# A gated recurrence feeding a balanced mixture of experts: the first expert's list apart, weights behind its rows, transposes ahead, matmuls dealt anew

## The chip, the cores and the metric

One core of a Trainium2 chip runs the whole kernel in one launch. The metric is the device time of an execution in microseconds (us); lower is better. The engines are named as in the profile: PE is TensorE's matmul (PEld its weight load), DVE is VectorE, ACT is ScalarE, POOL is GpSimd, and SP is the sync engine, which here issues loads from HBM.

## The reference

A gated linear recurrence over 4 batches, 8 heads, 768 tokens and head size 48 gives 3072 tokens of width 384. A layer of 8 experts follows, in which each token goes to exactly one expert and each expert takes exactly 384 tokens. All values are float32.

```python
f = 1.0 / (1.0 + np.exp(-f_logit))
for t in range(S):
    state = f[:, :, t, :, None] * state + np.einsum('bhd,bhe->bhde', k[:, :, t], v[:, :, t])
    y[:, :, t] = np.einsum('bhd,bhde->bhe', q[:, :, t], state)
x = y.transpose(0, 2, 1, 3).reshape(B * S, H * D)

logits = x @ w_gate                       # 3072 x 8
order = np.argsort(-logits.flatten())
for idx in order:                         # greedy: highest logit first
    tok, e = (int(idx) // E, int(idx) % E)
    if assigned[tok] >= 0 or counts[e] >= cap:     # cap = 3072 // 8 = 384
        continue
    assigned[tok] = e
    counts[e] += 1
for e in range(E):
    mask = assigned == e
    h = np.maximum(x[mask] @ w1[e], 0.0)  # 384 x 1024
    out[mask] = h @ w2[e]                 # 1024 x 384
```

## The kernel before

**Attention.** The recurrence is worked in 24 chunks of 128 tokens, as a software pipeline of seven stages (`attention`). The last stage, `gate`, computes a chunk's 8 logits and writes the row (384 outputs and 8 logits) to the DRAM tensor `xd`. SP loads the inputs of the chunks. SP's order is not written by hand; a scheduler places its instructions, while the orders of PE, DVE, ACT and POOL are written by hand in the expert phase (`tc.manual_schedule`).

**First list.** `search` finds, by 4 digits of 31 thresholds each, which tokens are above an expert's capacity bound for their first choice: DVE compares (`above`), PE counts (`cnt`), DVE takes the fullest expert (`most`, `filled`), and PE turns that into the next `base`. `positions` numbers the tokens within each expert, and `sort` produces the lists: DVE builds `numb` (which list column a token belongs to, times its number; 30 columns of 24) and `in_line` (which line of the list, in three parts), and 24 matmuls multiply them into `tokens`. The column order is 6 columns of left-over tokens (NL) and 3 per expert (TE). The result is rounded to integers in `tok`. `idle_turns(n)` puts n matmuls on a tile of ones into the PE queue whose result nobody reads.

**Gathers.** `fetch(e, i)` gathers the 128 rows of list column i of expert e from `xd` by an indirect DMA of POOL (196 KB, L534). POOL issues the two of expert 0, then six small gathers of the left-over tokens' logits (`lg`, L653), then two for each of experts 1 to 4.

**Weights.** `load_weights(e, ...)` issues w1 and w2 of an expert on SP (1536 KB each; L422 and L424). Experts 0 and 1 have space of their own (`early`) and are called for near the end of attention. Experts 2 to 4 use space that attention gives back. Experts 5 to 7 take over the tiles of experts 0 to 2 and are called for from the piece queue.

**Experts and routing side by side.** The left-over tokens are assigned in seven further rounds of `search`, whose chain runs back and forth between DVE and PE. Expert matmuls fill PE in between. An expert part (`ffn(e, first_block, n)`) is a list of pieces: n `turn`s (three transposes of gathered rows into a PSUM bank `Xe`, then an ACT copy to `xeT`, L486), 24 `up`s (three accumulate into a bank `H`, then an ACT Relu to `hT`, L498) and 8n `down`s (eight accumulate into `O`, then an ACT copy to `o`, L510, and POOL's scatter to the output, L511). `Xe` and `H` share three PSUM banks. Pieces wait in the deque `pe_work`, in the order of the parts: two blocks of each of experts 0 to 4, later the third blocks of these, then experts 5 to 7 whole.

The dealing is done when the program is built. A pair of clocks stands for PE and DVE. `V` adds an estimated DVE cost; `PE` is called ahead of each routing matmul, and first takes pieces as long as PE's clock stands behind DVE's:

```python
        def PE(cost):
            while pe_work and clock["pe"] + 0.2 < clock["dve"]:
                piece()
            clock["pe"] = max(clock["pe"], clock["dve"] + 0.05) + cost
            clock["dve"] = max(clock["dve"], clock["pe"] + 0.1)
```

When the lists are complete, a flag `beyond` is read by the engines (L762); it tells whether a general path must redo the work, which these inputs don't need. The remaining pieces then follow without routing between them.

Of the kernel before, what the change touches and what calls it, by code (L numbers as in the profile page):

```python
# [24 lines left out]
def kernel(  # L25
# [272 lines left out]
    def tt(out_, a, b, op):  # L298
        nc.vector.tensor_tensor(out=out_, in0=a, in1=b, op=op)
# [119 lines left out]

    def load_weights(e, pool, slot):  # L420
        w1 = pool.tile([128, DC, F], FP32, name="w1", tag=f"w1_{slot}", bufs=1)
        nc.sync.dma_start(out=w1[:], in_=moe_w1[e].rearrange("(c p) f -> p c f", p=128))  # L422
        w2 = pool.tile([128, FC, D], FP32, name="w2", tag=f"w2_{slot}", bufs=1)
        nc.sync.dma_start(out=w2[:], in_=moe_w2[e].rearrange("(c p) d -> p c d", p=128))  # L424
        slots[e] = (w1, w2)
# [3 lines left out]
    bounds(NCH - 1)  # L429
    overs(0, B, 0, NCH - 1)  # L430
    attention(ALL - 4, ALL - 1)
    load_weights(0, early, 0)
    first_choices(0, B - 1, NCH - 1, NCH)
    overs(0, B - 1, NCH - 1, NCH)
    attention(ALL - 1, ALL)
    load_weights(1, early, 1)
    first_choices(B - 1, B, NCH - 1, NCH)
# [5 lines left out]
    def fast():  # L443
# [12 lines left out]

        def V(cost=0.17):
            clock["dve"] += cost

        def PE(cost):  # L460
            while pe_work and clock["pe"] + 0.2 < clock["dve"]:
                piece()
            clock["pe"] = max(clock["pe"], clock["dve"] + 0.05) + cost
            clock["dve"] = max(clock["dve"], clock["pe"] + 0.1)

# [7 lines left out]
        def ffn(e, first_block, n):  # L473
# [27 lines left out]
            def down(i, ft):  # L501
                def go():
# [14 lines left out]

            return ([turn(i) for i in range(n)]
                    + [up(ft, d) for ft in range(FC) for d in range(DC)]
                    + [down(i, ft) for i in range(n) for ft in range(FC)])  # L520

        rows, lists = {}, {}

        def place_of(e, i):
            return NL + TE * (E - 1 - e) + i
# [13 lines left out]
        def search(over, choice, n, held):  # L539

            base = bank("base", "b")
            for d in range(DIGITS):
                above = rt([n, TH], f"above{n}", FP16)
                a, s = last_of(over, TH), mid_of(steps[d][:], n)
                if d == 0:
                    tt(above[:], a, s, ALU.is_ge)
                else:
                    stt(above[:], a, base[:, 0:1], s, ALU.subtract, ALU.is_ge)
                V(0.12 + n * TH / 960)
                r = bank("cnt", "r")  # L550
                PE(0.03 * n + 0.1)
                for c in range(n):
                    nc.tensor.matmul(out=r[0:TH, 0:E], lhsT=above[:, c, :], rhs=choice[:, c, :],  # L553
                                     start=(c == 0), stop=(c == n - 1 and held is None))
                if held is not None:
                    nc.tensor.matmul(out=r[0:TH, 0:E], lhsT=ones16[:, 0:TH], rhs=held[:],
                                     start=False, stop=True)
                most, filled = rt([1], "most"), rt([1], "filled", FP16)
                reduce(most[0:TH], r[0:TH, 0:E], ALU.max)
                ts(filled[0:TH], most[0:TH], CAP - 0.5, ALU.is_ge)  # L560
                V(0.35)
                PE(0.06)
                nc.tensor.matmul(out=base[:, 0:1], lhsT=units[d][0:TH, :], rhs=filled[0:TH],
                                 start=(d == 0), stop=(d == DIGITS - 1), skip_group_check=True)
            return base

        def positions(kind, nk, n, code, notfirst_, held):
# [9 lines left out]
                                         op0=ALU.mult, op1=ALU.add)  # L577
            V(0.1 + w / 400)
            PE(0.2)
# [13 lines left out]
            stt(line[:], q[:], -128.0, pos[:], ALU.mult, ALU.add)  # L593
            tt(blk[:], q[:], code, ALU.add)
            return total, line, blk

        def sort(line, blk, val, blocks_, n, nq, part):

            numb = rt([nq, n], f"numb{n}", FP16)
            tt(numb[:], mid_of(blk[:], nq), blocks_, ALU.is_equal)  # L600
            tt(numb[:], numb[:], mid_of(val, nq), ALU.mult)
            V(0.2 + nq * n / 960)
            r = bank("tokens", "r")
            in_line = rt([n // 2, 128, 2], f"in_line{n}", FP16, 1)
            lp = line[:].rearrange("p (c j) -> p c j", j=2)
            for c0 in range(0, n // 2, part):
                tt(in_line[:, c0:c0 + part], lp[:, c0:c0 + part].unsqueeze(2).to_broadcast(
                    (128, part, 128, 2)), mid_of(pairs[:], part), ALU.is_equal)
                V(0.12 + part * 256 / 1900)
                PE(0.03 * 2 * part)  # L610
                for c in range(2 * c0, 2 * (c0 + part)):
                    nc.tensor.matmul(out=r[:, 0:nq], lhsT=in_line[:, c // 2, :, c % 2],
                                     rhs=numb[:, :, c], start=(c == 0), stop=(c == n - 1))
            return r

# [9 lines left out]
        with tc.manual_schedule(engines=engines):  # L625
# [10 lines left out]
            idle_turns(12)  # L636
            r = sort(line, blk, value[:], blocks[:], NT, NQ, 4)
            idle_turns(6)
            found, tok = rt([NQ], "found", FP32, 1), rt([NQ], "tok", I32, 1)
            ts(found[:], r[:, 0:NQ], -1024.0, ALU.max, 2047.0, ALU.min)  # L640
# [3 lines left out]
               float(1024 * (DX // E) + D // E), ALU.add)  # L644
            for e in range(NA):
                for i in range(2):
                    p = place_of(e, i)
                    lists[e, i] = tok[:, p:p + 1]
            fetch(0, 0)
            fetch(0, 1)  # L650
            lg = rt([NL, E], "lg", FP32, 1)
# [9 lines left out]

            clock.update(pe=6.0, dve=0.0)
            for e in range(NA):
                if e >= 2:
                    load_weights(e, pools[e], e)
                pe_work.extend(ffn(e, 0, 2))

# [14 lines left out]
            nc.vector.memset(got[:], 0.0)  # L682
            clock["dve"] = 14.0
            ts(lg[:], lg[:], low_scale[:, 0:1], ALU.add, low_scale[:, 1:2], ALU.mult)
            tt(lg[:], lg[:], last_of(gone[:], E), ALU.add)
            for rnd in range(1, E):
# [3 lines left out]
                tt(ch[:], lg[:], last_of(ov[:], E), ALU.is_equal)  # L690
                V(0.55)
# [4 lines left out]
                V(0.4)  # L696
                if rnd == E - 1:
# [3 lines left out]
                tt(now[:], held[:], more[:], ALU.add)  # L701
                V(0.35)
                PE(0.1)
                m2 = bank("m2", "r")
# [5 lines left out]
                tt(lg[:], lg[:], last_of(gone[:], E), ALU.add)  # L710
                V(0.7)

# [4 lines left out]
            tt(kind2[:], mid_of(code2[:], E), kinds[:, 1:KC, 0:NL], ALU.is_equal)  # L717
            V(0.6)
# [4 lines left out]
            r = sort(line2, blk2, val_l[:], blocks[:, NL:NQ, 0:NL], NL, NQ - NL, 3)  # L723
            tok2 = rt([NQ - NL], "tok2", I32, 1)
# [4 lines left out]
            for e in range(E):  # L729
                for i in range(2 if e < NA else 0, TE):  # L730
                    p = place_of(e, i) - NL
                    lists[e, i] = tok2[:, p:p + 1]
            ends = bank("ends", "r")
            nc.tensor.matmul(out=ends[:, 0:E], lhsT=ones16[:], rhs=total[:, 1:KC], start=True,
# [8 lines left out]
            reduce(twice[:], times[:], ALU.max)  # L743
            stt(span[:], twice[:], 1.5, span[:], ALU.is_ge, ALU.add)
            nc.tensor.matmul(out=ends[:, E:E + 1], lhsT=onesf[:], rhs=span[:], start=True,
                             stop=True)
# [599 lines left out]
```

## Time and profile before

| | |
|---|---|
| median of 3 runs | 510.9 us (507.04 to 511.99) |
| the profiled execution | 509.44 us, span from first to last instruction 507.5 us |
| PE busy | 460.7 us, 91% of the span |
| DVE, ACT, POOL busy | 156.4, 135.8, 106.3 us |
| mean granted TensorE clock | 0.965 |
| weight loads | 16 of 1536 KB on SP |

Times in the views count from the span's first instruction. "Busy" of PE is the time in which at least one matmul is under way. In the profile's slices each digit is a share in tenths of one fortieth of the span (12.7 us); "PEclk" is the clock granted to TensorE. A view of the timeline gives start, duration, engine, line, operation and the tiles written and read, and in brackets how long the engine was idle before and what ended that. A view of waits gives the waiting engine and line, then what it waited for, with total time, number of times and the longest.

### The profile page before, as it was taken

To read this page: it belongs to the slowest core of one execution; us is meant where nothing else is said; L and a number is where in the kernel's file an instruction comes from. 1 tells how busy PE (TensorE), PEld (TensorE's weight loads), DVE (VectorE), ACT (ScalarE), POOL (GpSimd) and SP (SyncE) were. 2 spreads that over 40 slices of the span, in tenths; PEclk is the share of its full clock that TensorE was granted. 3 is DMA by queue.
4 is the path that set the end of the run, shared out by engine and by line. 5 is a ranking of instruction groups with operands and counts; after the bars stand their busy time and mean duration, and the time that the engine had idled before them with its cause. 6 is when DMAs were issued, how large, how long until landed. Compare 5 with 4: busy or idle time off the path is not lost.

```text
span 507.5 us, 11617 instructions
## 1 busy us (share of the span) xinstructions
PE 460.7 (91%) x4972; PEld 325.3 (64%) x4972; DVE 156.4 (31%) x503; ACT 135.8 (27%) x365; POOL 106.3 (21%) x157
## 2 busy tenths in 40 slices
PE   2999999999999486899997899999999999999991
PEld 1778888888888345546554576867777555555550
DVE  6466666666668551244455000000000000000000
ACT  3446554554432001102011021312222220312200
POOL 3133333333221027200010400012330001001010
PEclk9999999999999685999999899999999999999996
DMA  8976997999911598200000300005992000000000
GB/s 173 201 159 141 198 197 153 193 242 265 336 65 48 215 392 268 67 17 17 0 32 1 83 31 16 17 31 188 325 337 103 16 0 31 17 16 31 1 30 22
DMA packets 118541, 59.28 MB, mean 117 GB/s; under 512 B 101840, under 2 KB 113104, under 8 KB 118480
## 3 DMA queue, kind: packets, MB, share of 16 engines
q1 hardware_dynamic: 111760, 44.06, 33.2%
q0 software_dynamic: 3264, 9.56, 5.6%
q10 hardware_dynamic: 3456, 4.82, 2.7%
q8 instruction: 41, 0.67, 0.5%
q14 instruction: 20, 0.16, 0.1%
HBM read 48.89 MB, written 9.54 MB: 115 GB/s over the span
## 4 chain that ended last, share of the span: by engine, by line
PE 62%; issue 26%; POOL 4%; DVE 3%; ACT 1%; DMA 1%; POOLq 0%; ACTq 0%; DVEq 0%
PE H L494 17%; PE O L505 14%; PE Y L225 5%; PE T L171 4%; PE A L208 4%; PE L L139 3%; PE Y L235 3%; PE L L143 2%; PE X L249 2%; PE dS L190 2%; POOL out_dram L511 2%; PE cnt L553 2%; PE X L260 2%; DMA xe<-xd,tok 1%; ACT xeT L486 1%
## 5 line engine op out<-in xcount | busy, mean ns | idle before, releaser
L494 PE MATMUL H<-xeT,w 128*128 128x256 f32 (+2 forms) x624 | 142.2, 381 | 9.5 <-ACT xeT L486 8.1
L505 PE MATMUL O<-w,hT 128*128 128x384 f32 x384 | 131.9, 492 | 0.0
L494 PEld LDWEIGHTS H<-xeT,w 128*128 128x128 f32 x624 | 99.6, 195 | 38.8 <-ACT xeT L486 11.1
L505 PEld LDWEIGHTS O<-w,hT 128*128 128x128 f32 x384 | 70.8, 190 | 43.8 <-issue 1.0
L511 POOL DMA_INDIRECT out_dram<-o,tok x24 | 23.5, 979 | 235.6 <-ACT o L510 224.9
L498 ACT ACTIVATE hT<-H 128x256 f32<-128x256 f32 (+2 forms) x104 | 37.7, 368 | 120.9 <-PE H L494 118.6
L510 ACT COPY o<-O 128x384 f32<-128x384 f32 x24 | 11.5, 479 | 122.1 <-PE O L505 122.1
L213 DVE COPY_PREDICATED am<-mask,A 128x512 f32<-128x512 int32 x48 | 32.4, 729 | 29.9 <-PE A L208 29.9
L534 POOL DMA_INDIRECT xe<-xd,tok x24 | 23.1, 963 | 52.3 <-DVE few L673 29.9
L163 POOL TENSOR_TENSOR kg<-k,ek 128x384 f32<-128x384 f32 x24 | 25.8, 1073 | 27.7 <-ACT ek L151 21.9
L139 PE MATMUL L<-g,wcum 128*128 128x384 f32 x48 | 23.0, 563 | 7.4 <-DVE linef L333 7.4
L225 PE MATMUL Y<-v,am 128*64 128x48 f32 x768 | 27.5, 224 | 0.0
L225 PEld LDWEIGHTS Y<-v,am 128*64 128x64 f32 x768 | 24.4, 138 | 3.9 <-issue 3.7
L208 PE MATMUL A<-qT,kT 48*64 48x128 f32 x768 | 26.7, 278 | 0.0
L143 PEld LDWEIGHTS L<-ind,g 128*64 128x64 f32 x384 | 13.9, 144 | 14.1 <-issue 14.1
L208 PEld LDWEIGHTS A<-qT,kT 48*64 48x64 f32 x768 | 21.5, 137 | 0.2
L553 PEld LDWEIGHTS <-above 128*31 128x31 f16 x264 | 8.8, 97 | 18.3 <-DVE above L306 13.3
L150 ACT ACTIVATE eq<-dl 128x384 f32<-128x384 f32 x24 | 12.5, 523 | 28.5 <-DVE dl L148 27.9
L148 DVE TENSOR_SCALAR dl<-L 128x384 f32<-128x384 f32 x24 | 13.4, 557 | 20.5 <-PE L L143 20.5
L171 PE MATMUL T<-ident,qg 128*128 128x128 f32 x96 | 16.6, 299 | 1.8 <-DVE qg L162 1.8
L486 ACT COPY xeT<-Xe 128x384 f32<-128x384 f32 x24 | 10.8, 487 | 27.9 <-PE Xe L483 27.8
L157 POOL TENSOR_TENSOR gl<-spans 128x4 f32<-128x4 f32 x20 | 4.0, 201 | 67.8 <-DVE logits L265 40.1
(178 smaller groups left out, 456.9 us busy)
## 6 DMA issues: line engine op xcount, KB each, us to landing
w<-in_moe_w_dram SPq DMA_DIRECT2D x16, 1536.0 KB, 9.7
xd<-x ACTq DMA_DIRECT2D x24, 196.0 KB, 3.1
f<-in_f_logit_dram SPq DMA_DIRECT2D x24, 192.0 KB, 4.0
q<-in_q_dram SPq DMA_DIRECT2D x24, 192.0 KB, 4.1
k<-in_k_dram SPq DMA_DIRECT2D x24, 192.0 KB, 4.0
v<-in_v_dram SPq DMA_DIRECT2D x24, 192.0 KB, 4.2
xe<-xd,tok POOLq DMA_INDIRECT x24
out_dram<-o,tok POOLq DMA_INDIRECT x24
```

The source lines that it names most:

```text
L139: nc.tensor.matmul(out=Lv, lhsT=wcum[:], rhs=g[:, :, 0:DH], start=True, stop=True)
L143: nc.tensor.matmul(out=ends[DP * r:DP * r + DP, :, hp], lhsT=g[:, 2 * hp + r, :], rhs=ind[:], start=True, stop=True)
L163: nc.gpsimd.tensor_tensor(out=kg[:, :, 0:DH], in0=G["k"][:], in1=ek[:], op=ALU.mult)
L171: nc.tensor.transpose(out=T[:, 128 * hp:128 * hp + 128], in_=t[:, 2 * hp:2 * hp + 2, :].rearrange("t h d -> t (h d)"), identity=ident[:])
L208: nc.tensor.matmul(out=A[par][HC * j:HC * j + HC, 128 * hp:128 * hp + 128], lhsT=G["kT"][rows, hp, HC * j:HC * j + HC], rhs=G["qT"][rows, ...
L213: nc.vector.copy_predicated(am[:, par], mask[:].unsqueeze(1).to_broadcast((128, HP, 128)), A[par][:].rearrange("s (a t) -> s a t", t=128))
L225: nc.tensor.matmul(out=Y[par][HC * j:HC * j + HC, DH * hp:DH * hp + DH], lhsT=G["am"][:, par, hp, HC * j:HC * j + HC], rhs=G["v"][:, 2 * h ...
L494: nc.tensor.matmul(out=L["H"][:, 0:w], lhsT=slots[e][0][:, d, 128 * ft:128 * ft + 128], rhs=xT[:, d, 0:w], start=(d == 0), stop=(d == DC - 1))
L498: nc.scalar.activation(out=hT[:, ft, 0:w], in_=L["H"][:, 0:w], func=AF.Relu)
L505: nc.tensor.matmul(out=L["O"][:, 0:D], lhsT=hT[:, ft, 128 * i:128 * i + 128], rhs=slots[e][1][:, ft, :], start=(ft == 0), stop=(ft == FC - 1))
L511: nc.gpsimd.indirect_dma_start(out=outs[next(tiles)][:, :], out_offset=bass.IndirectOffsetOnAxis(ap=token(e, first_block + i), axis=0), in ...
L534: nc.gpsimd.indirect_dma_start(out=t[:], out_offset=None, in_=xd[:, :], in_offset=bass.IndirectOffsetOnAxis(ap=token(e, i), axis=0))
```

## The change

The change has five parts.

1. Expert 0's two list columns are sorted first, from `numb` of two columns, and its two gathers are issued from them; the full sort follows and uses the same `in_line` tile again.
2. `load_weights` takes an argument `behind`: ACT then copies one element of a gathered row into the w1 tile before the load may write it. Expert 1's w1 is loaded so, behind expert 0's second gather, and the call for expert 1 stands with those for experts 2 to 4. The call for expert 0 stands four chunks earlier.
3. `add` puts the turns of a part ahead of the last three pieces of the queue, with one older piece between two turns, and the rest of the part at the end. The gathers of experts 5 to 7 are put into the queue 28 pieces before the end of what stands before their part.
4. The costs of `V` and `PE` and the clocks' starting values are replaced, and some calls are added or moved.
5. `numbers` is split off `sort`.

```diff
-    def load_weights(e, pool, slot):
+    def load_weights(e, pool, slot, behind=None):
         w1 = pool.tile([128, DC, F], FP32, name="w1", tag=f"w1_{slot}", bufs=1)
+        if behind is not None:
+            nc.scalar.copy(out=w1[0:1, 0, 0:1], in_=behind)
         nc.sync.dma_start(out=w1[:], in_=moe_w1[e].rearrange("(c p) f -> p c f", p=128))
...
+    load_weights(0, early, 0)
     attention(ALL - 4, ALL - 1)
-    load_weights(0, early, 0)
...
     attention(ALL - 1, ALL)
-    load_weights(1, early, 1)
...
-        def V(cost=0.17):
-            clock["dve"] += cost
+        def V(n=1, cost=0.21):
+            clock["dve"] += n * cost

         def PE(cost):
-            while pe_work and clock["pe"] + 0.2 < clock["dve"]:
+            while pe_work and clock["pe"] < clock["dve"] + 0.1:
                 piece()
-            clock["pe"] = max(clock["pe"], clock["dve"] + 0.05) + cost
-            clock["dve"] = max(clock["dve"], clock["pe"] + 0.1)
+            clock["pe"] = max(clock["pe"], clock["dve"] + 0.1) + cost
+            clock["dve"] = max(clock["dve"], clock["pe"] + 0.22)
...
-            return ([turn(i) for i in range(n)]
-                    + [up(ft, d) for ft in range(FC) for d in range(DC)]
+            return ([turn(i) for i in range(n)],
+                    [up(ft, d) for ft in range(FC) for d in range(DC)]
                     + [down(i, ft) for i in range(n) for ft in range(FC)])
+
+        AHEAD_OF = 3
+
+        def add(parts):
+            turns, rest = parts
+            at = max(0, len(pe_work) - AHEAD_OF - (len(turns) - 1))
+            for t in turns:
+                pe_work.insert(at, t)
+                at += 2
+            pe_work.extend(rest)
...
-                V(0.12 + n * TH / 960)
+                V(cost=0.15 + n * TH / 700)
...
-                V(0.35)
+                V(2)
...
-            r = sort(line, blk, value[:], blocks[:], NT, NQ, 4)
+            p0 = place_of(0, 0)
+            r, in_line = sort(line, numbers(blk, value[:], blocks[:, p0:p0 + 2], NT, 2), NT, 2, 4)
             idle_turns(6)
+            tok0 = rt([2], "tok0", I32, 1)
+            found0 = rt([2], "found0", FP32, 1)
+            ts(found0[:], r[:, 0:2], -1024.0, ALU.max, 2047.0, ALU.min)
+            ts(tok0[:], found0[:], 1024.0, ALU.add)
+            for i in range(2):
+                lists[0, i] = tok0[:, i:i + 1]
+                fetch(0, i)
+            r, _ = sort(line, numbers(blk, value[:], blocks[:], NT, NQ), NT, NQ, 12, in_line)
...
-            for e in range(NA):
+            for e in range(1, NA):
...
-            fetch(0, 0)
-            fetch(0, 1)
...
-            clock.update(pe=6.0, dve=0.0)
+            clock.update(pe=4.0, dve=0.0)
             for e in range(NA):
-                if e >= 2:
-                    load_weights(e, pools[e], e)
-                pe_work.extend(ffn(e, 0, 2))
+                if e:
+                    load_weights(e, pools[e], e, rows[0, 1][0:1, 0:1] if e == 1 else None)
+                add(ffn(e, 0, 2))
...
-            clock["dve"] = 14.0
+            clock["dve"] = 15.0
...
+            V(3)
+            PE(0.1)
             ends = bank("ends", "r")
...
+            V(6)
+            PE(0.1)
             nc.tensor.matmul(out=ends[:, E:E + 1], lhsT=onesf[:], rhs=span[:], start=True,
                              stop=True)
...
             for e in range(NA):
                 fetch(e, 2)
-                pe_work.extend(ffn(e, 2, 1))
+                add(ffn(e, 2, 1))
                 if NA + e < E:
                     pe_work.append((0.0, lambda e=e: load_weights(NA + e, pools[e], e)))
-                    pe_work.append((0.0, lambda e=e: [fetch(NA + e, i) for i in range(TE)]))
             for e in range(NA, E):
-                pe_work.extend(ffn(e, 0, TE))
+                at = max(0, len(pe_work) - 28)
+                pe_work.insert(at, (0.0, lambda e=e: [fetch(e, i) for i in range(TE)]))
+                add(ffn(e, 0, TE))
```

More of the change, by code (lines that the diff above doesn't have):

```diff
@@ L577, in positions @@
                                          op0=ALU.mult, op1=ALU.add)
-            V(0.1 + w / 400)
+            V(cost=0.1 + w / 350)
             PE(0.2)
@@ L594, in positions, with numbers, sort @@
             tt(blk[:], q[:], code, ALU.add)
+            V(9)
             return total, line, blk
-        def sort(line, blk, val, blocks_, n, nq, part):
-            numb = rt([nq, n], f"numb{n}", FP16)
+        def numbers(blk, val, blocks_, n, nq):
+            numb = rt([nq, n], f"numb{n}_{nq}", FP16, 1)
             tt(numb[:], mid_of(blk[:], nq), blocks_, ALU.is_equal)
             tt(numb[:], numb[:], mid_of(val, nq), ALU.mult)
-            V(0.2 + nq * n / 960)
+            V(cost=0.3 + nq * n / 700)
+            return numb
+        def sort(line, numb, n, nq, part, in_line=None):
             r = bank("tokens", "r")
-            in_line = rt([n // 2, 128, 2], f"in_line{n}", FP16, 1)
+            ready = in_line is not None
+            if not ready:
+                in_line = rt([n // 2, 128, 2], f"in_line{n}", FP16, 1)
             lp = line[:].rearrange("p (c j) -> p c j", j=2)
             for c0 in range(0, n // 2, part):
-                tt(in_line[:, c0:c0 + part], lp[:, c0:c0 + part].unsqueeze(2).to_broadcast(
-                    (128, part, 128, 2)), mid_of(pairs[:], part), ALU.is_equal)
-                V(0.12 + part * 256 / 1900)
+                if not ready:
+                    tt(in_line[:, c0:c0 + part], lp[:, c0:c0 + part].unsqueeze(2).to_broadcast(
+                        (128, part, 128, 2)), mid_of(pairs[:], part), ALU.is_equal)
+                    V(cost=0.15 + part * 256 / 1700)
                 PE(0.03 * 2 * part)
@@ L613, in sort @@
                                      rhs=numb[:, :, c], start=(c == 0), stop=(c == n - 1))
-            return r
+            return r, in_line
         engines = {mybir.EngineType.PE, mybir.EngineType.DVE, mybir.EngineType.Activation,
@@ L690, in fast @@
                 tt(ch[:], lg[:], last_of(ov[:], E), ALU.is_equal)
-                V(0.55)
+                V(3, 0.23)
                 base = search(ov[:], ch, NL, held)
@@ L695, in fast @@
                 tt(got[:], got[:], sure[:], ALU.add)
-                V(0.4)
+                V(2)
                 if rnd == E - 1:
@@ L701, in fast @@
                 tt(now[:], held[:], more[:], ALU.add)
-                V(0.35)
-                PE(0.1)
+                V(2)
+                PE(0.05)
                 m2 = bank("m2", "r")
@@ L710, in fast @@
                 tt(lg[:], lg[:], last_of(gone[:], E), ALU.add)
-                V(0.7)
+                V(4)
             codes, code2 = rt([NL, E], "codes"), rt([NL], "code2", FP16)
@@ L717, in fast @@
             tt(kind2[:], mid_of(code2[:], E), kinds[:, 1:KC, 0:NL], ALU.is_equal)
-            V(0.6)
+            V(3)
             nf2 = rt([E, NL], "nf2", FP16, 1)
@@ L722, in fast @@
                                             nf2[:].rearrange("p k c -> p (k c)"), total[:, 1:KC])
-            r = sort(line2, blk2, val_l[:], blocks[:, NL:NQ, 0:NL], NL, NQ - NL, 3)
+            numb2 = numbers(blk2, val_l[:], blocks[:, NL:NQ, 0:NL], NL, NQ - NL)
+            r, _ = sort(line2, numb2, NL, NQ - NL, 3)
             tok2 = rt([NQ - NL], "tok2", I32, 1)
@@ L732, in fast @@
                     lists[e, i] = tok2[:, p:p + 1]
+            V(3)
+            PE(0.1)
             ends = bank("ends", "r")
```

## The prediction

> **What bounds the kernel now.** I read the summary of the span first, then the engine windows, the chain of waits of TensorE, and the timelines of SP, POOL and PE around 170 to 200 us.
>
> ```profile
> span 507.5 us, 11617 instructions
> ...
> PE 460.7 (91%) x4972; PEld 325.3 (64%) x4972; DVE 156.4 (31%) x503; ACT 135.8 (27%) x365; POOL 106.3 (21%) x157
> ...
> PE   2999999999999486899997899999999999999991
> ...
> PEclk9999999999999685999999899999999999999996
> ```
>
> TensorE (PE) is busy 91% of the span, so only what PE does, waits for, or does at a lower clock can move the end. Attention fills PE up to 160 us, and the experts fill it from 196 us to the end. The time to be had lies in the dip at 160 to 200 us, in the gaps of the experts, and in the slices whose clock is below 9.
>
> ```profile
> 170.09 0.37 SPq L422 DMA_DIRECT2D w<-in_moe_w_dram  x1
> 173.46 8.18 SPq L422 DMA_DIRECT2D w<-in_moe_w_dram  x1
> 181.67 1.33 SPq L424 DMA_DIRECT2D w<-in_moe_w_dram  x1
> ...
> 186.68 1.15 POOL L534 DMA_INDIRECT xe<-xd,tok  x1 [29.91 <-DVE few L673]
> ...
> 193.60 0.90 PE L483 MATMUL Xe<-ident,xe 128*128 128x128 f32 x3 [4.48 <-DMA xe<-xd,tok]
> 194.81 0.90 PE L483 MATMUL Xe<-ident,xe 128*128 128x128 f32 x3 [0.31 <-DMA xe<-xd,tok]
> 196.28 1.22 PE L494 MATMUL H<-xeT,w 128*128 128x256 f32 x2 [0.57 <-ACT xeT L486]
> ```
>
> Six weight loads (experts 2 to 4, 1536 KB each) leave SP from 170 us, and expert 0's first gather leaves POOL at 186.68, into that traffic. PE stands idle 4.48 us for the rows. The first expert matmul starts at 196.28.
>
> ```profile
> 182.00:192.00 10.00, 6.59 (x55) 3.97 (x52) 3.79 (x16) 0.00 (x0) 4.10 (x5) 1.00 1.04 392
> 192.00:193.00 1.00, 0.00 (x0) 0.00 (x0) 0.00 (x0) 0.00 (x0) 0.82 (x1) 0.60 1.02 385
> 193.00:202.00 9.00, 7.53 (x20) 5.52 (x21) 1.50 (x6) 1.54 (x4) 6.74 (x8) 0.50 0.79 241
> 202.00:203.00 1.00, 1.00 (x5) 0.85 (x4) 0.00 (x0) 0.18 (x1) 0.82 (x1) 0.78 0.62 169
> 281.00:284.00 3.00, 3.00 (x8) 2.37 (x9) 0.00 (x0) 0.38 (x1) 2.08 (x4) 0.50 0.64 182
> ```
>
> The last three columns are granted clock, DMA share and GB/s. After the idle time the clock is 0.50: a mean of 0.60 in 192 to 193 and 0.78 in 202 to 203 puts the half clock from 192.2 to 202.4. It comes again for 281 to 284, after the gaps at the end of routing.
>
> ```profile
> PE H L494 <- ACT xeT L486: 8.1, 13, 0.8
> PE ends L745 <- DVE span L306: 1.7, 1, 1.7
> PE base L563 <- DVE filled L303: 1.4, 1, 1.4
> PE H L494 <- DVE beyond L752: 1.3, 1, 1.3
> PE tokens L612 <- DVE in_line L299: 1.3, 1, 1.3
> ```
>
> This is all that PE waits for from 196 us on (total, times, longest). Each of the 13 expert parts begins with a wait for ScalarE's copy of its transposed rows.
>
> **What the Trainium skill says.** "TensorE: Matmul & The Clock Gate" (What's actually happening): the clock halves after an idle window of about 3.4 us and returns after a busy one, on a free-running grid. The trace agrees: the cold stretch of 10.2 us is three such windows. "DMA: Bandwidth & Descriptors" (Issuing engines are not separate DMA queues): all issuers share 16 engines. The trace agrees: the first gather took from 186.68 to about 193.5 (6.9 us) beside 370 to 417 GB/s, while five gathers issued at 278.89 to 283.99, beside no weights, end their traffic before 287, under 3 us from issue to landing. The same page (Anatomy of one DMA — SWDGE) prices 196 KB at about 2.0 + 0.45 us, close to that.
>
> **Part 1, the first list by itself.** Today two products of 128x720 (0.53 us each) stand ahead of the in_line products. They become 128x48, for which I take 0.18, as the 128x48 f16 rows (0.18 for kind, L299). That saves 0.7 us, so the gathers leave at about 185.95 and 187.4. The full list follows while POOL issues them: two products (1.1), 24 small matmuls (8 took 0.44 us of weight loads, so about 1.3), and two DVE steps. It ends near 188.0, so the six lg gathers start near 189.0, against 189.38. On PE 24 matmuls are added, followed by the same 18 idle turns (3.1 us at 0.17): PE is free at about 190.5. That now sets the earliest start.
>
> **Part 2, other weights behind the rows.** The order of the built program's SP queue shows that this is only partly so: expert 1's w2 keeps an early place in attention, w1 and w2 of experts 2 and 3 still leave at 170, and only expert 1's w1, then expert 4's pair, stand behind the ACT copy that needs the rows. So 4 x 1536 KB = 6.3 MB move first instead of 9.4. At 392 GB/s from about 172 they end near 188, where before they ran to 197. The gathers meet at most 1 us of that: I put the rows at 189.3 and 190.4. The 1x1 ACT copy (about 0.2) waits for those rows with the two xeT copies behind it, which need them anyway: nothing. With Xe at 190.6, two times 0.5 warm, and the last copy 0.5, H starts at 192.3 instead of 196.28: **4.0 us**. If the gathers are as slow as before, only 0.7 remains. Behind the waiting SP instruction stand expert 4's loads and the flag read; expert 1's w1 should land by 198 and is needed near 219.
>
> **Part 3, the clock.** Idle turns, transposes and ups now follow with gaps of some 0.6 us, so the window before H is busy. Before, 196.28 to 202.4 ran at half speed: 6.1 us, half of it won, **3.1**. If the grid falls badly, nothing.
>
> **Part 4, dealing by measured durations.** In the changed program two pieces, not one, stand between a count and its base and between base and next count; nearly 11.3 us of ups and downs precede the first count (24 x 0.443 + 0.65). Two ups of 0.443 exceed the DVE answer of 0.6 to 0.9 us. The number of switches, about 0.74 us for a count and base pair, stays. At the end, 2.3 us of DVE (own to in_line) lie beside eight ups (3.5), and the span chain (1.7) beside seven ups. The 1.3 and 1.7 waits go: **3.0**. The flag wait of 1.3 stays, as no piece precedes it. Without the gaps the half clock of about 3.4 us at 281 goes: **1.7**. The 1.4 at the first count is not explained by DVE's work, which was ready at 201.6: between 0 and 1.4, I take **0.7**. The routing lasts longer, up to expert 4's ups, with 13 downs (8.4 us) left to cover the third lists' gathers: no new wait.
>
> **Part 5, transposes ahead.** All waits for xeT but the first, 8.1 - 0.57 = 7.5 us in 12 places, are covered by three downs (3 x 0.65, against 0.62 to 0.78). I leave 0.05 each for the switch: **6.9**. Gathers of experts 5 to 7 move to 28 pieces before their part. For expert 5 POOL issues them from 2 us into the previous part and they land at 5 to 7.4, and PE wants them from 7.6: tight but covered, and the later two have 16 us of downs.
>
> Sum: 4.0 + 3.1 + 3.0 + 1.7 + 0.7 + 6.9 = 19.4. The profiled execution took 509.44 us (span 507.5), so 490.0. The median of the three runs, 510.9, is 1.5 above it; I forecast **491.5**.
>
> **Rivals.** (a) The gathers stay late, because 6.3 MB still go ahead of them, and the clock falls as before: 19.4 - 7.1 + 0.7 = 13.0, thus 497.9. For it: the loads at 170 keep their places. Against: their end near 188. (b) The transposes or the dealing only trade one wait for another, an H bank or late rows: without part 5, 12.5, thus 498.4. (c) Slower: expert 1's first up waits for the w1 now tied to the rows. Each microsecond after 219 costs one; it passes the gain only if w1 lands after 238, and is slower by 1% after 243. With 1536 KB at 390 GB/s from 191 it would need a queue standing still for 45 us. Little speaks for it.
>
> **Numbers.** Forecast 0.70, (a) 0.18, (b) 0.08, (c) 0.04. About 1% (5 us) is what a measurement tells from no change. Cases main, (a) and (b) are faster by more than that save for small tails: faster 0.93, same 0.04, slower 0.03. Range: the low end takes the whole 1.4, no switch cost and no offset to the median (some 488) and 2 for costs not seen: 486. The high end takes in (a) and (b) with 1.5 more: 500.
>
> **What would show it.** Right: first H near 192.3, no clock below 1 from there to the end of the experts, no xeT wait above 0.2, one gap of 1.3 at the flag. Wrong: Xe waiting for rows after 192, a cold stretch at 192 to 202, waits of PE on DVE in the searches, or on a weight load at expert 1 or on rows at expert 5.

## The result and the profile after

| | before | after |
|---|---|---|
| median of 4 executions | 509.66 us (507.04 to 511.99) | 487.62 us (486.62 to 488.32) |
| ratio, after to before | | 0.957, 95% interval 0.951 to 0.962 |
| the profiled execution | 509.44 us, span 507.5 | 487.56 us, span 485.7 |
| from the first compare of the search to the first expert matmul | 168.30 to 196.28: 27.98 us | 169.45 to 194.18: 24.73 us |

The forecast was 491.5 us: 490.0, which is 19.4 below the profiled execution of before, and 1.5 for a median that then stood at 510.9. With a fourth execution that median is 509.66. The span fell by 21.8. Parts are numbered here and below as the prediction numbers them: 1 is the first list, 2 the weights, 3 the clock, 4 the dealing, 5 the turns (transposes) ahead. The lines of the summary that answer to those shown of before, from the page of the changed kernel:

```profile
span 485.7 us, 11676 instructions
...
PE 454.8 (94%) x4996; PEld 323.1 (67%) x4996; DVE 157.2 (32%) x507; ACT 138.1 (28%) x366; POOL 105.2 (22%) x157
...
PE   2999999999999859999999999899999999999991
...
PEclk9999999999999857999999999999999999999996
```

PE has 24 more matmuls (the first list's), yet is busy for 5.9 us less. From 194 us on no slice of the clock is below 9, but for the last. Work of TensorE now takes 73% of the chain of waits and "issue" 15%, where it was 62% and 26% before.

The start of the experts, from the timelines of the queues (start, duration, engine, line, operation):

```profile
186.85 1.14 POOL L545 DMA_INDIRECT xe<-xd,tok  x1 [29.24 <-DVE numb L299]
188.23 4.61 PE L641 MATMUL nothing<-idle,ones 128*128 128x384 f16 x18
...
192.45 0.19 ACT L423 COPY w<-xe 1x1 f32<-1x1 f32 x1 [23.43 <-DMA xe<-xd,tok]
192.67 0.91 SPq L424 DMA_DIRECT2D w<-in_moe_w_dram  x2
192.70 0.85 PE L484 MATMUL Xe<-ident,xe 128*128 128x128 f32 x6
...
194.18 10.63 PE L495 MATMUL H<-xeT,w 128*128 128x256 f32 x48 [0.62 <-ACT xeT L487]
204.32 0.31 DVE L303 TENSOR_SCALAR lg<-lg,low_scale 128x48 f32<-128x48 f32 x1 [10.62 <-DMA lg<-xd,at_l]
```

The line of the kernel before that answers to the last of these:

```profile
199.97 0.37 DVE L303 TENSOR_SCALAR lg<-lg,low_scale 128x48 f32<-128x48 f32 x1 [9.99 <-issue]
```

The rows are there at 192.45, when the one-element copy of part 2 runs, and PE leaves its idle turns at the same time, so no wait for rows is left. Expert 1's w1 and expert 4's pair go out behind that copy. The left-over tokens' logits (`lg`) are worth keeping in mind: they are first used at 204.32, where before it was 199.97.

The clock, from the windows of the same kernel (busy time of PE, PEld, DVE, ACT and POOL, then granted clock, DMA share, GB/s):

```profile
182.00:187.00 5.00, 4.54 (x42) 2.61 (x41) 4.13 (x14) 0.00 (x0) 0.15 (x1) 0.75 1.03 394
...
188.00:191.00 3.00, 3.00 (x17) 1.57 (x15) 0.53 (x5) 0.00 (x0) 2.09 (x3) 0.50 0.92 296
...
193.00:202.00 9.00, 8.38 (x42) 7.23 (x40) 0.63 (x6) 2.78 (x7) 6.62 (x7) 1.00 0.94 241
...
281.00:284.00 3.00, 3.00 (x19) 2.15 (x19) 0.92 (x5) 0.41 (x2) 0.00 (x0) 1.00 0.02 5
```

The half clock now falls on idle turns (187.9 to 191.3 us), whose work nobody needs. 193 to 202 us, 0.79 before, has the whole clock, and so has 281 to 284, 0.50 before.

All waits of PE from 180 to 480 us (total, times, longest):

```profile
PE H L495 <- DVE beyond L783: 1.4, 1, 1.4
PE H L495 <- ACT xeT L487: 0.6, 1, 0.6
PE cnt L564 <- DVE above L299: 0.5, 1, 0.5
PE tokens L631 <- DVE numb L299: 0.5, 1, 0.5
```

Of the 13 waits for transposed rows one is left. The flag wait stayed, as forecast. The wait of the first count is new: it is for `lg`.

Below, "time beyond pace" is used for what a view of waits can't give. PE's matmul records follow each other at a fixed pace where nothing holds them: 0.216 us a record for an up of 256 columns (0.112 at 128, 0.3225 at 384), 0.3225 for a down, 0.109 for a transpose, two records for each up or down. I took the distance from each record's start to the next one's and subtracted that pace; distances that start at a routing matmul count in full. From the first up to the last down this sum is 44.5 us before (33.25 up to the flag, 11.24 behind it) and 24.8 after (24.78 and 0.04). The difference, 19.7, and the 2.1 us by which the first up comes earlier make the 21.8 of the span.

### The profile page after: what moved, and what is told of

Its sections match the earlier page's. It is cut to its first block, busy times and chain, and to the rows that moved or that the text cites. A ratio compares the mean times of both kernels' runs of the same rounds, so it can differ in the third digit from the quotient of the medians.

```text
span 485.7 us, 11676 instructions
## 1 busy us (share of the span) xinstructions
PE 454.8 (94%) x4996; PEld 323.1 (67%) x4996; DVE 157.2 (32%) x507; ACT 138.1 (28%) x366; POOL 105.2 (22%) x157
## 4 chain that ended last, share of the span: by engine, by line
PE 73%; issue 15%; POOL 4%; DVE 4%; DMA 2%; ACT 0%; POOLq 0%; DVEq 0%
PE O L506 20%; PE H L495 19%; PE Y L225 5%; PE T L171 4%; PE A L208 4%; PE L L139 4%; PE L L143 3%; PE Y L235 2%; PE dS L190 2%; PE X L249 2%; PE cnt L564 2%; PE X L260 2%; DMA lg<-xd,at_l 2%; PE Xe L484 1%; POOL out_dram L512 1%
## 5 line engine op out<-in xcount | busy, mean ns | idle before, releaser
L495 PE MATMUL H<-xeT,w 128*128 128x256 f32 (+2 forms) x624 | 135.2, 369 | 2.0 <-DVE beyond L783 1.4
L506 PE MATMUL O<-w,hT 128*128 128x384 f32 x384 | 136.6, 494 | 0.0
L495 PEld LDWEIGHTS H<-xeT,w 128*128 128x128 f32 x624 | 97.7, 191 | 28.9 <-issue 1.6
L506 PEld LDWEIGHTS O<-w,hT 128*128 128x128 f32 x384 | 68.8, 190 | 37.0 <-issue 0.4
L163 POOL TENSOR_TENSOR kg<-k,ek 128x384 f32<-128x384 f32 x24 | 25.6, 1067 | 26.7 <-ACT ek L151 20.9
L487 ACT COPY xeT<-Xe 128x384 f32<-128x384 f32 x24 | 11.4, 478 | 44.0 <-PE Xe L484 44.0
L564 PEld LDWEIGHTS <-above 128*31 128x31 f16 x264 | 8.8, 97 | 19.0 <-issue 10.5
L150 ACT ACTIVATE eq<-dl 128x384 f32<-128x384 f32 x24 | 12.6, 523 | 27.7 <-DVE dl L148 27.2
```

The lines of the kernel that those rows point to most:

```text
L163: nc.gpsimd.tensor_tensor(out=kg[:, :, 0:DH], in0=G["k"][:], in1=ek[:], op=ALU.mult)
L495: nc.tensor.matmul(out=L["H"][:, 0:w], lhsT=slots[e][0][:, d, 128 * ft:128 * ft + 128], rhs=xT[:, d, 0:w], start=(d == 0), stop=(d == DC - 1))
L506: nc.tensor.matmul(out=L["O"][:, 0:D], lhsT=hT[:, ft, 128 * i:128 * i + 128], rhs=slots[e][1][:, ft, :], start=(ft == 0), stop=(ft == FC - 1))
```

## The experiments

The kernel before was measured beside every kernel. Its median was 509.66 us beside the changed kernel, and 509.05, 508.46 and 513.73 in three groups of experiments. The first three lie within 1.2 us, and kernels of these are compared directly; those of the last group (the final four) only with each other. The three groups ran on three different chips.

### Turns back at the head of their part

```diff
-            at = max(0, len(pe_work) - AHEAD_OF - (len(turns) - 1))
-            for t in turns:
-                pe_work.insert(at, t)
-                at += 2
-            pe_work.extend(rest)
+            pe_work.extend(turns + rest)
```

> The changed kernel with the turns of each part again right ahead of the part's own ups; all else as changed. Theory: a part's start costs 0.85 us of PE (the wait for the copy, and the drain of the last transposes that the wait view does not count), in 10 parts without routing, and about 0.5 in 2 to 3 parts beside routing: some 9 us more, about 496.5. Rival, the price of the prediction: the listed waits alone, 6.9 us, about 494.5. Second rival: the copies are mostly hidden elsewhere, under 3 us more.

Measured: 498.38 us, ratio to before 0.980 (0.975 to 0.985); 10.8 above the changed kernel. The view of waits and two lines of PE's timeline of this kernel:

```profile
PE H L495 <- ACT xeT L487: 8.1, 13, 0.8
...
304.65 0.55 PE L484 MATMUL Xe<-ident,xe 128*128 128x128 f32 x3
305.77 0.70 PE L495 MATMUL H<-xeT,w 128*128 128x256 f32 x2 [0.57 <-ACT xeT L487]
```

The waits come back as they were. But they are shown too short. Three transposes at their pace take 0.33 us; they are shown with 0.55, as the end of a matmul in the trace is modelled, and only what follows that end is called a wait. From start to start, a part's beginning costs 0.85 us beyond pace up to its first up (6.76 us in 8 of them without routing between), and the second record of that up comes another 0.10 late. At that rate the twelve starts that the change covers would cost 11.4 us, somewhat less where routing stands between. A little of the 10.8 isn't theirs: the wait at the first count is 1.2 in this trace, not 0.5.

### The turns ahead alone

The kernel before, with `add` and the earlier gathers of experts 5 to 7 and nothing else:

```diff
-                pe_work.extend(ffn(e, 0, 2))
+                add(ffn(e, 0, 2))
...
-                pe_work.extend(ffn(e, 2, 1))
+                add(ffn(e, 2, 1))
...
+                at = max(0, len(pe_work) - 28)
+                pe_work.insert(at, (0.0, lambda e=e: [fetch(e, i) for i in range(TE)]))
+                add(ffn(e, 0, TE))
```

> The kernel before with the turns ahead and the later gathers moved, and nothing else of the change. If the parts of the change add up: 9 us less than before, about 500.5 (theory), or 6.9 less, about 502.8 (the prediction's price). If turns ahead need the new dealing to pay, less than 5.

Measured: 497.65 us, 0.982 (0.974 to 0.989), 11.4 below before. Taken out or put in alone, part 5 is worth about 11 us, half of the whole; the intervals leave 3 to 4 us to either side. The stall of 1.4 us at the first base isn't in this trace, so part of the 11.4 may be that. The waits of PE for `ends` (1.7), `in_line` (1.3), the flag (1.3) and the first rows (4.8 in two) stay, and the half clock too (192.8 to 199.6 and 274.7 to 281.5).

### The old dealing

Part 4 undone: the costs and clock values of before, everything else as changed, for instance

```diff
-            while pe_work and clock["pe"] < clock["dve"] + 0.1:
+            while pe_work and clock["pe"] + 0.2 < clock["dve"]:
...
-            clock["dve"] = 15.0
+            clock["dve"] = 14.0
```

> The changed kernel with all costs of the dealing as before. Theory: only the waits of PE in the view of before come back (1.4 at a base, 1.3 at the last list, 1.7 at the span) and about 1.6 of half clock after them: 4 to 6 us more, about 492.5, and the pair of count and base costs about 0.76 us of PE with one piece or two between. Rival: one up is too short to cover DVE's answer, which hides in each switch; then 8 us or more.

Measured: 502.78 us, 0.987 (0.984 to 0.990), 15 above the changed kernel: far more than the theory, and not for the rival's reason, a price paid in each switch. From its timelines of DVE and PE and its windows:

```profile
207.29 0.31 DVE L303 TENSOR_SCALAR lg<-lg,low_scale 128x48 f32<-128x48 f32 x1 [12.10 <-DMA lg<-xd,at_l]
208.88 0.32 PE L564 MATMUL cnt<-ch,above 128*31 128x8 f16 x6 [4.73 <-DVE above L299]
209.00:220.00 11.00, 11.00 (x49) 5.72 (x48) 3.38 (x16) 1.15 (x3) 0.73 (x1) 0.50 0.72 258
```

The old dealing puts 17 ups ahead of the first count. They end before `lg` is there, PE stands for 4.73 us, and the half clock follows for 13.65 us (208.0 to 221.6), though PE is busy in every microsecond of it that the window shows. In this execution (505.15 us) the time beyond pace is 40.05 us against 24.8.

### Weights back at their old places

Part 2 undone: experts 0 and 1 called for as before, no load behind rows.

```diff
...
-                if e:
-                    load_weights(e, pools[e], e, rows[0, 1][0:1, 0:1] if e == 1 else None)
+                if e >= 2:
+                    load_weights(e, pools[e], e)
```

> The changed kernel with the weight loads of experts 0 and 1 at their old places and no copy ahead of a load; the first list stays by itself. Theory: expert 0's gathers meet 9.4 MB again, the first expert matmul comes 2 to 3 us later and meets the half clock, 3 us: about 5 us more, 492.5. Rival: the idle turns ahead of the first transposes (until 192.5 in the changed kernel) set the start and the rows arrive beside them: 0 to 1 us more. In either case the left-over logits should land near 200 instead of 204.

Measured: 489.85 us, 0.965 (0.959 to 0.971), 2.2 above the changed kernel, with overlapping intervals. PE waits 1.5 us for rows and starts the experts 26.68 us behind the search's start, not 24.73; but `lg` comes early and no count waits.

### One list

Part 1 undone: one sort of all 30 columns ahead of the first gather.

```diff
-            r, in_line = sort(line, numbers(blk, value[:], blocks[:, p0:p0 + 2], NT, 2), NT, 2, 4)
+            r, in_line = sort(line, numbers(blk, value[:], blocks[:], NT, NQ), NT, NQ, 4)
...
```

> The changed kernel with one sort of all 30 columns ahead of expert 0's gathers, as before; weights, turns and dealing as changed. Theory: the gathers leave about 0.7 us later and the rows set the start, so 1 to 1.5 us more, about 489. Rival: without the second set of 24 matmuls the idle turns end 1.5 us sooner and the start does not move: 0 to 0.5 us more.

Measured: 489.06 us, 0.960 (0.957 to 0.964), 1.4 above the changed kernel, again with overlapping intervals. The time itself doesn't settle it; the trace does: the first gather leaves 18.4 us behind the first compare in all three traces with one list that I read for it (before 18.38, the turns alone 18.37, this one 18.39), and 17.4 in those with the first list apart (17.40 in the changed kernel, 17.41 with the turns back, 17.40 with the old dealing and with the old weights). So part 1 is worth 1.0 us at the gather. What that is worth at the end is less clear. In this trace the first up comes only 0.3 us later, counted from the search's start, but PE has waited 2.1 us for rows, and the half clock covers 192.1 to 199.0, some 4.9 us of ups at half speed.

### Old dealing and old weights together

The edits of the two sections above in one kernel, so that parts 2 and 4 can be set against each other.

> The changed kernel with the old dealing and with the weight loads at their old places (first list and turns as changed). Theory: the 15 us that the old dealing cost with the weights behind the rows came mostly from the left-over logits, which landed 4 us later beside those weights while only 17 ups stood ahead of the first count, and from the half clock after that wait; with the old places they land near 200 and that wait is gone: about 496.5, some 6 us faster than with the moved weights. Rival: the old dealing itself costs the 15 us wherever the weights stand: about 504.

Measured: 496.63 us, 0.980 (0.974 to 0.985). The four kernels in a square (medians, us):

| | weights behind rows | weights at old places |
|---|---|---|
| new dealing | 487.6 | 489.9 |
| old dealing | 502.8 | 496.6 |

The same move of the weights gains 2.2 us under the new dealing and loses 6.1 under the old one. The intervals of the ratios overlap at their edges in each pair, so the traces carry it. What goes with it is the time from the issue of expert 0's second gather to the first use of `lg`, whose gathers follow it:

| kernel | expert loads going out behind rows | us |
|---|---|---|
| before; turns alone | none | 11.8; 11.9 |
| old weights, new dealing; old dealing | none | 12.6; 12.9 |
| after; turns back; old dealing; one list | expert 1's w1, expert 4's pair | 16.0; 15.9; 16.0; 16.1 |

Three loads of 1536 KB, released when the rows are there, meet the six small gathers that follow: they come some 3 to 4 us later. That the loads are the cause is tested below, where they are moved behind these gathers. The new dealing has 24 ups and a down ahead of the first count, not 17 ups, and so hides it but for 0.5 us. Under either dealing the move brings the experts' start nearer to the search's (24.7 and 24.1 us, against 26.7 and 26.8).

### The old dealing with a longer front

```diff
-            clock["dve"] = 14.0
+            clock["dve"] = 17.35
```

This is the kernel with the old dealing, in which one starting value is changed so that 24 ups and a down stand ahead of the first count there as well.

> The changed kernel with the old dealing, but with DVE's clock ahead of the first count set so that the same 24 ups and one down stand ahead of it as in the changed kernel. Theory: the wait of 4.7 us at the first count and the half clock after it go, and what stays of the old dealing is its waits at the last list and the span (1.3 and 1.7) and the half clock behind them (1.8 and more): 5 us above the changed kernel, about 493. Rival: one piece between count and base costs PE in each of the 28 steps: 8 us or more above, about 496.

Measured: 492.78 us, 0.968 (0.964 to 0.972), 10 below the kernel with 14.0. Of the 15 us of the old dealing 10 are thus one wait and its cold clock at the front. The other 5 lie in what follows, which is not taken apart further: the waits for `ends` 1.7, at the first count 1.2 and for `tokens` 1.3 are there, and half clock for 277.4 to 280.8.

### Weights behind the logits, and work ahead of the flag

If loads that meet the `lg` gathers are the cost of part 2, they should stand behind those. Here the pairs of experts 2 to 4 are called for from the piece queue with the copy taken from the last of the left-over logits; expert 1's w1 stays behind the rows. As the trace shows, only the w1 of the three wait for that copy; their w2 leave at 171 us. Some ups are also dealt ahead of the flag read.

```diff
-                if e:
-                    load_weights(e, pools[e], e, rows[0, 1][0:1, 0:1] if e == 1 else None)
+                if e == 1:
+                    load_weights(e, pools[e], e, rows[0, 1][0:1, 0:1])
                 add(ffn(e, 0, 2))
+                if e == 0:
+                    pe_work.insert(22, (0.0, lambda: [
+                        load_weights(o, pools[o], o, lg[0:1, NL - 1, 0:1]) for o in range(2, NA)]))
...
+            V(6)
+            PE(0.0)
             flag = nc.values_load(beyond[0:1, 0:1], min_val=0, max_val=3072)
```

> The changed kernel with two more moves: w1 of experts 2 to 4 loaded behind the last gather of the left-over logits (their ACT copies stand among expert 0's ups), and three pieces dealt ahead of the flag's read. Theory: 4.7 instead of 6.3 MB go ahead of the rows, so the start comes about 1 us sooner; the logits land near 200 again and the 0.5 at the first count goes; the 1.4 at the flag goes: 2.5 to 3 us less, about 485. Rival: the rows' own way (4.1 us from issue) does not shrink, or the copies hold up ACT: only the flag's 1.4, about 486.3, or more than now.

Measured: 484.82 us (482.65 to 486.36), 0.954 (0.949 to 0.959), in the same group as the last three. From its timelines of SP, PE and DVE:

```profile
190.91 11.11 SPq L424 DMA_DIRECT2D w<-in_moe_w_dram  x4
192.02 10.63 PE L495 MATMUL H<-xeT,w 128*128 128x256 f32 x48 [0.62 <-ACT xeT L487]
199.23 0.31 DVE L303 TENSOR_SCALAR lg<-lg,low_scale 128x48 f32<-128x48 f32 x1 [7.68 <-DMA lg<-xd,at_l]
```

The first of the four loads, expert 1's w1, leaves at 190.91, the other three from 200.57. Behind `lg` these three no longer meet it: it comes 11.6 us after the gather's issue, as early as in the kernel before, and the first count doesn't wait. So one load released behind the rows costs `lg` nothing that shows. The experts start 23.2 us behind the search's start. The flag wait is gone, and there is no half clock from the first transposes to the end of the experts.

### The changed kernel again, and three relatives beside it

The same kernel as changed, measured together with the next three, so that their small differences could be told.

> The changed kernel unaltered, as the measure for the other three on the same chip: about 487.6.

Measured: 498.29 us (496.78 to 501.85), 0.970 (0.967 to 0.974). The kernel before had 513.73 in this group, 4 to 5 more than in the others, and the changed one had 10.7 more. Its timeline of ACT and its view of PE's waits:

```profile
209.30 0.94 ACT L499 ACTIVATE hT<-H 128x256 f32<-128x256 f32 x3 [8.14 <-remote]
...
PE H L495 <- ACT hT L499: 5.7, 1, 5.7
PE H L495 <- issue: 3.0, 1, 3.0
```

ACT doesn't take the ups' results for 8.14 us while the gathers of experts 1 to 4 are under way; PE waits 5.7 us for the banks that ACT has to read, and the half clock follows (207.0 to 213.8). The 3.0 us stand ahead of the first up, at 195.60, and the half clock covers 196.8 to 200.2 as well. The time beyond pace is 9.1 more than in the execution shown above (33.95 against 24.82) and the first up comes 1.4 later, which makes 10.5 of the 10.7. What holds ACT, the trace doesn't say; "remote" means that the profile has no instruction for the release. So the change gains 15.4 us here, 3.0%, where it gained 22 before; the two intervals don't meet.

Work ahead of the flag alone (only the `V(6)` and `PE(0.0)` of the kernel above):

> The changed kernel with only three pieces dealt ahead of the flag's read. Theory: the wait of 1.4 us there goes and nothing else moves, 1.4 us below the changed kernel. Rival: the pieces are missed later, at the first third block, and nothing is gained.

Measured: 495.94 us, 0.967 (0.963 to 0.971), 2.4 below the changed kernel beside it. The flag wait is gone from the view of waits; the size is not settled, since the intervals overlap and the stall at the front differs from execution to execution.

All w1 loads of experts 1 to 4 behind the rows:

```diff
-                    load_weights(e, pools[e], e, rows[0, 1][0:1, 0:1] if e == 1 else None)
+                    load_weights(e, pools[e], e, rows[0, 1][0:1, 0:1])
```

> The changed kernel with w1 of experts 2 to 4 behind expert 0's rows as well (their w2 still leave early, so 4.7 MB go ahead of the rows and 6.3 MB behind them). Theory: the rows come 1 to 1.5 us sooner, but the left-over logits stand beside all of the 6.3 MB and land near 207; PE waits about 4 us at the first count and may fall to the half clock: 2 to 6 us above the changed kernel. Rival: only the bytes ahead of the rows count: 1 to 1.5 us below it.

Measured: 497.93 us, 0.970 (0.965 to 0.974), the same as the changed kernel beside it, where more was expected. `lg` came 15.5 us behind the gather's issue with four loads behind the rows, no later than with three. PE waited 4.4 us for ACT at the start and 4.8 again later, the same stall, so the time says little; that more loads delay `lg` more is not borne out.

Weights behind the logits, again:

> The kernel with w1 of experts 2 to 4 behind the logits and the flag's read covered, once more beside the changed kernel: 2.5 to 3 us below it on the same chip if its gain is real; within 1 us of it if 484.8 was the chip.

Measured: 496.36 us (492.36 to 498.48), 0.965 (0.962 to 0.968), 1.9 below the changed kernel beside it, with intervals that overlap a little. `lg` came after 11.8 us here too, and the stall of ACT (8.09 us, to 204.73) was here as well. Set against each other across groups (484.8 and 487.6) or within one (496.4 and 498.3), this version is the lower by 2 to 3 us; that is less than these measurements settle.

## Why the prediction was right, point by point

The forecast, 491.5, missed the median by 3.9 us and the gain in the span by 2.4; the rest is the 1.5 added for the median. Against the steps, with time beyond pace from the two traces:

| step | predicted | measured |
|---|---|---|
| parts 1 and 2, earlier first up | 4.0 | 2.1 (3.25 from the search's start) |
| part 3, half clock at the first ups | 3.1 | 3.0 |
| part 4, waits for `ends` and `in_line` | 3.0 | 3.4 |
| part 4, half clock behind the routing | 1.7 | 1.7 |
| part 4, stall at the first base ("first count" in the prediction) | 0.7 | 1.5 |
| part 5, starts of parts | 6.9 | 10.4 |
| wait at the first count | 0 | -0.5 |
| what is left, small distances | 0 | 0.2 |
| sum | 19.4 | 21.8 |

The sum is closer than its terms: the start gave 1.9 us too much and the first count 0.5, and part 5 gave 3.5 too little. That these offset each other is luck.

**Part 5 was the mis-sized term.** Twelve waits were taken at what the view of waits gives them, 7.5 us in all, less 0.05 each. From start to start, ten of them cost 8.53 us in the kernel before up to the first up, and 1.0 more inside these ups; the two in the routing cost 0.9. Behind the flag nothing is left of it in the changed kernel (0.04), so the switch cost there is nothing either. The two experiments that undo it or do it alone give 10.8 and 11.4. The trace agrees with the working on the gathers of experts 5 to 7: no wait for their rows is in the view.

**The start was 0.7 us later than worked out.** From the first compare, 24.0 were predicted (192.3 less 168.30) and 24.73 came. The gather did leave a microsecond earlier (0.7 predicted). But the rows took 4.15 us from the second issue to the copy (188.30 to 192.45), not 3, and the 18 idle turns took 4.61 us and not 3.1, since half clock fell on them. The four loads ahead of the rows had not ended near 188: the last landed at 190.33. With the weights behind the logits there are three, the last landed at 186.57, and the rows then took 3.04 us from the second issue to the copy (187.65 to 190.69), as forecast. "DMA: Bandwidth & Descriptors" of the Trainium skill (Issuing engines are not separate DMA queues), by which the transfers of all issuers run on the same 16 engines, agrees: both gathers took 5.6 us from the first issue beside what was left of four loads (296 GB/s in 188 to 191), where the first alone took 6.9 beside six. Another 1.15 us of the absolute start come from the search's own start, 168.30 against 169.45; over the traces read here the search starts between 167.3 and 172.5, with either placing of the weights, so it isn't put to the change.

**The clock came out as forecast, but its rule only in part.** The half clock at 192 to 202 and at 281 went with the gaps ahead of it. "TensorE: Matmul & The Clock Gate" (What's actually happening) has windows of about 3.4 us, and the stretches here last 3.4, 6.8, 10.2 and 13.65 us, whole multiples. By the same section an idle window halves the clock and a busy one restores it; with that the traces agree only in part. In the changed kernel the clock halves at 187.9, though PE shows as busy for 2.95 of the 3.41 us before; with the old dealing it stays at half through 211.4 to 218.2, two windows that PE fills, and on to 221.6. That the stretch in the changed kernel ends 2.8 us ahead of the first up is in part luck: in three of the four traces of the last group one covers the first ups.

**What stayed.** The flag wait, 1.3 before and 1.4 after, was rightly expected to stay. A count and base pair costs 0.76 us beyond pace in both traces, near the 0.74 of the prediction.

**What was missed.** Part 2 was said to leave nothing waiting but SP's own queue. It overlooked who shares the DMA engines with expert 1's w1 and expert 4's pair: the `lg` gathers, 4 us later than before. That wait of PE on DVE, one of the prediction's signs of being wrong, did come. The price was 0.5 us only because part 4 puts 24 ups and a down ahead of the first count; the square of four kernels shows it at 6.1 us without that. The prediction had listed the front of 11.3 us under part 4, for another purpose.

**The rivals.** (a), late gathers and a cold clock, and (b), one wait traded for another, would each have left 498; PE's waits in the changed kernel sum to 3.0 us, and its clock is whole from the first up to the end of the experts. The changed kernel did take 498 in the last group, but by the stall of ACT, which no rival had. (c), a wait for expert 1's w1, doesn't appear at all: the load landed at 200.40.

Taken in one order, the four steps from 509.1 give: turns ahead to 497.7, the first list apart to 496.6 (with the old weights), the new dealing to 489.9, the weights behind rows to 487.6. The steps of 1 and 2 us are within their intervals, and the kernels are of different groups.

## What to carry to other kernels

A repeated start-up wait is priced from the start of one matmul to the start of the next, not from the view of waits, which counts only behind a modelled end. When a load is held back so that it doesn't meet one gather, look for the next small gather in time: it inherits the traffic, and whoever waits for it pays. Ahead of an arrival that may be late, more covering work than the mean is worth having, because one wait of a few microseconds can cost the clock for much longer: 4.73 us of waiting were followed by 13.65 us of half clock.

## What the runs showed of the hardware that was not expected

A wait of 4.73 us of PE was followed by 13.65 us of half clock, though PE was busy meanwhile with small routing matmuls between expert matmuls; elsewhere, after waits of 4.4 to 6.0 us, it was 3.4 to 10.2 us.

In all four kernels of the third group ACT stood for 5 to 8 us with PE's results ready, with "remote" as the releaser, while POOL's row gathers were in flight. In the profiled execution of the kernel before, ACT and DVE resume together (208.71 and 208.83 us), which may be the same thing in a weaker form: it would be the stall of 1.41 us at the first base. Neither its cause nor why one group had it and the others hardly did was settled; no run took the gathers away. The kernels of the other groups had the same gathers in flight without it, and the group with the stall ran on another chip than the two before it, so the chip is one open rival.
